# Running sums of the first two head pairs made in short runs, and the opening steps in another order

## Chip, core and metric

The kernel runs on one core of a Trainium2 chip. The metric is the device time of one execution in microseconds (us). The engines are named as in the profile: PE is the matrix engine TensorE, PEld its weight loads, DVE VectorE, ACT ScalarE, POOL GpSimd, SP the engine whose queue issues nearly all the DMAs.

## The reference, cut to what matters

Causal attention over 8 batches of 8 heads (576 positions, 64 wide), with a bias made from running sums of `s`; its output goes into a mixture of four experts, each an attention of its own, of which two are kept per position.

```python
cum = np.cumsum(np.maximum(s, 0.0), axis=-1)
bias = -(cum[:, :, :, None] - cum[:, :, None, :])
scores = np.where(causal, -1e9, q @ k.T / 8 + np.minimum(bias, 0.0))
attn = softmax(scores) @ v
x = attn.transpose(0, 2, 1, 3).reshape(B, S, H * D)
# then, for each expert e: softmax(causal(x @ wq[e] @ (x @ wk[e]).T / 8)) @ (x @ wv[e]) @ wo[e],
# weighted by a softmax over the two largest of x @ w_gate
```

## The kernel before

The 64 heads are worked in pairs, and so are the experts' attentions: 50 slots in all, 0 to 49. For a pair, the program makes the row maxima of the scores, then the scores and their exponentials, then the product with v. The scores of a pair are two products that add up: one (L688) over the low parts of q and k, the other (L693) over their high parts with extra rows below row 64. In those rows K2 holds the running sum of `s`, split into three terms that TensorE takes without loss, against rows of ones in Q2; one more row of Q2 holds minus the row maximum, against a row of ones in K2. So the running sum must be in place before a pair's maxima (L626), and the maxima before its scores. Q2 and K2 are rings of three buffers (`fill`, L349, sets their constant rows); Q1 and K1, with the low parts, are rings of two.

The order of the program is written out by hand in `STEPS`: a step `n:x` is step x of slot n, and each engine takes what it is given in that order. Steps that the prediction names, with the pair that slot n works on:

- `z0` to `z47`: an idle product on TensorE (L1340) whose result nothing reads; `FIRST_IDLE` such products stand ahead of all steps.
- `ld`, `lv`: loads of q and k (pair n+3) and of v (pair n). `hc` (pair n+2): running sums to K2 by DMA. `h0` to `h3` (pair n+2): high parts of q and k, on ACT.
- `lq`, `lk`, `l0`, `l1` (pair n+1): low parts. `lq` copies q on POOL, `lk` copies k on ACT, and `l0`, `l1` subtract (on DVE, and on POOL for one pair).
- `m0` to `m2` (pair n+2), `m3` to `m5` (pair n+1): maxima products, one PSUM bank each; `M0` to `M5` reduce the bank on DVE and give it back. `mt`, `mA`, `mq` (pair n+1): the maxima turned by TensorE, copied by ACT, and sent by two DMAs to the row of Q2.
- `s0` to `s6` and `E0` to `E6`: scores and their exponentials (pair n); `v0` to `v7`: product with v (pair n-1). `f1`, `f2`: `fill` of ring buffers 1 and 2. `cu` (slot -1): running sums to DRAM, for the pairs from 2 on. `lc`: constants, on POOL.

So pair 0 opens with slot -2, and `0:s4` is its first score product, `1:s4` that of pair 1. The running sums of all 64 heads are made at once (`running_sums`, L416): 64 partitions of 576 elements each, one scan along each of them on DVE, then the split in three.

Of the kernel before, what the change touches and what calls it, by code (L numbers as in the profile page):

```python
# [17 lines left out]
P = 128  # L18
# [12 lines left out]
FIRST_IDLE, IDLE = 32, 48  # L31
# [49 lines left out]
def heads(t, at, c0, c1):  # L81
# [240 lines left out]

COPY_Q, COPY_K = 3, 9

FB = [0, 8, 10, 12]
NQK1 = 2
NQK2 = 3
RC = 96
RM = 96


@with_exitstack
def tile_attention_then_moe(ctx, tc, qk, vm, vt, s, wqk, wvg, wo, out):
    nc = tc.nc
# [61 lines left out]
    def late_constants():  # L396
# [3 lines left out]
        for i in range(3):  # L400
            nc.gpsimd.memset(VB[i][64:128, :, 4], 0.0)
# [929 lines left out]
    def call(items):  # L1331
        for x in items:
            x()
# [118 lines left out]
```

## Time and profile before

| | us |
|---|---|
| median of 3 runs | 640.03 |
| lowest and highest run | 639.34, 640.57 |
| the profiled execution | 639.84 |
| its span, first to last instruction | 638.1 |
| PE busy in the span | 631.2 (99%) |
| DVE, ACT, POOL busy | 513.8, 445.2, 428.4 |

PE counts as busy also while it runs idle products, so the 99% tells nothing of useful work. The profile has a chain of work that ended last (followed back from the last instruction), a timeline of each engine, and windows that count one line's instructions in a stretch.

### The profile page before, as it was taken

The page shows a single profiled execution, that of the slowest core. Times are in us where ns is not written, and L with a number is a line of the kernel's source. Part 1 is how long each engine was busy: PE and PEld are TensorE (multiplying, and loading weights), DVE is VectorE, ACT ScalarE, POOL GpSimd, SP SyncE. Part 2 cuts the span into 40 slices and gives each one's busy share as a digit, 9 for nine tenths or more (in the row PEclk, how much of TensorE's full clock was granted, in tenths as well). Part 3 has the DMA queues.
Part 4 walks back from the last instruction along what each step waited for, and adds up shares of the span by engine and source line. Part 5 has one row for each costly group of instructions (what it writes and reads, how often), then busy time and mean ns, then how long its engine had stood idle before and what let it go on. Part 6 is the DMA issues. An engine that isn't in the chain of part 4 may idle for free.

```text
span 638.1 us, 16517 instructions
## 1 busy us (share of the span) xinstructions
PE 631.2 (99%) x5962; PEld 539.8 (85%) x5962; DVE 513.8 (81%) x1440; ACT 445.2 (70%) x974; POOL 428.4 (67%) x530
## 2 busy tenths in 40 slices
PE   9999999999999999999999999999999999999997
PEld 9888989789888888788897898788888889788875
DVE  8789788877989978895888778798887978763784
ACT  6697768866876676776768766785676776576354
POOL 8866598769864977487667766588676676828030
PEclk9999999999999999999999999999999999999999
DMA  5464643563565357445634454572563643432404
GB/s 167 132 186 133 182 111 79 143 141 96 159 162 136 91 150 188 145 130 134 182 100 132 129 130 134 156 200 76 141 193 87 157 130 88 111 101 64 103 1 148
DMA packets 61160, 83.39 MB, mean 131 GB/s; under 512 B 27063, under 2 KB 35623, under 8 KB 61079
## 3 DMA queue, kind: packets, MB, share of 16 engines
q1 hardware_dynamic: 60934, 82.21, 47.9%
q8 instruction: 47, 0.77, 0.5%
q14 instruction: 35, 0.28, 0.1%
q10 hardware_dynamic: 144, 0.13, 0.1%
HBM read 44.61 MB, written 10.16 MB: 86 GB/s over the span
## 4 chain that ended last, share of the span: by engine, by line
PE 97%; ACT 2%; DVE 1%; issue 0%; ACTq 0%
PE pvp L845 21%; PE pq L1080 16%; PE s L688 13%; PE s L693 12%; PE mx L626 10%; PE pw L1080 7%; PE po L1080 7%; PE sm L895 4%; PE idle L1340 3%; PE po L1049 1%; PE mt L661 1%; PE pw L1135 1%; PE pw L1140 1%; PE es L795 1%; PE gt L1249 0%; ACT p L709 0%
## 5 line engine op out<-in xcount | busy, mean ns | idle before, releaser
L709 ACT ACTIVATE p<-s 128x512 f32<-128x512 f32 x288 | 159.3, 589 | 40.8 <-PE s L693 32.3
L640 DVE CUSTOM_DVE_ANT_0 unread<-mx,mask 128x256 uint8<-128x256 f32 (+6 forms) x384 | 142.2, 419 | 33.9 <-PE mx L626 32.9
L688 PE MATMUL s<-q,k 128*128 128x288 f32 (+5 forms) x672 | 167.0, 285 | 0.5 <-issue 0.3
L693 PE MATMUL s<-q,k 97*128 97x288 f32 (+5 forms) x672 | 159.9, 279 | 0.0
L727 POOL TENSOR_SCALAR_AFFINE_SELECT p<-p 128x256 f32<-128x256 f32 (+2 forms) x183 | 109.5, 600 | 70.1 <-ACT p L709 67.7
L688 PEld LDWEIGHTS s<-q,k 128*128 128x128 f32 (+1 forms) x672 | 122.5, 183 | 7.5 <-issue 3.5
L774 POOL TENSOR_TENSOR r<-r,p 128x640 f32<-128x640 f32 x84 | 120.7, 1437 | 6.8
L693 PEld LDWEIGHTS s<-q,k 97*128 97x128 f32 (+1 forms) x672 | 121.7, 183 | 0.8
L845 PE MATMUL pvp<-p,v 128*64 128x320 f32 (+6 forms) x1024 | 99.5, 334 | 0.0
L600 DVE TENSOR_TENSOR q<-raw,q 64x576 fp32r<-64x576 f32 (+1 forms) x86 | 81.1, 952 | 22.5 <-ACT q L560 7.9
L605 DVE TENSOR_TENSOR k<-raw,k 64x576 fp32r<-64x576 f32 (+1 forms) x86 | 84.4, 991 | 5.5 <-DMA k<-k 3.4
L845 PEld LDWEIGHTS pvp<-p,v 128*64 128x64 f32 x1024 | 68.9, 136 | 22.7 <-ACT p L709 0.9
L626 PE MATMUL mx<-k,q 96*64 96x320 bf16 (+7 forms) x960 | 82.3, 293 | 0.9 <-DVE mcol L640 0.6
L1080 PE MATMUL pq<-xh,wqkh 128*128 128x288 f32 x256 | 76.4, 299 | 0.0
L1080 PE MATMUL pq<-xl,wqkh 128*128 128x288 f32 x256 | 75.6, 295 | 0.0
L1080 PE MATMUL pq<-xh,wqkl 128*128 128x288 f32 x256 | 75.4, 294 | 0.0
L768 POOL TENSOR_TENSOR r<-p 128x128 f32<-128x128 f32 x37 | 22.2, 600 | 72.3 <-ACT p L709 72.3
L626 PEld LDWEIGHTS <-q 96*64 96x64 bf16 x960 | 48.1, 109 | 22.1 <-issue 6.6
L563 ACT ACTIVATE k<-raw 64x576 fp32r<-64x576 f32 x96 | 64.8, 680 | 2.7 <-DMA raw<-in_qk_dram 0.6
L560 ACT ACTIVATE q<-raw 64x576 fp32r<-64x576 f32 x96 | 64.7, 681 | 1.9 <-PE s L693 0.4
L859 ACT ACTIVATE pv<-pvp 128x256 f32<-128x256 f32 (+1 forms) x92 | 36.1, 402 | 36.4 <-PE pvp L845 35.6
L1098 ACT ACTIVATE raw<-pq 128x288 f32<-128x288 f32 x64 | 25.4, 404 | 35.1 <-PE pq L1080 35.1
(159 smaller groups left out, 1265.5 us busy)
## 6 DMA issues: line engine op xcount, KB each, us to landing
raw<-in_qk_dram SPq DMA_DIRECT2D x30, 576.0 KB
rb<-rr SPq DMA_DIRECT2D x92, 144.0 KB
q<-q SPq DMA_DIRECT2D x45, 288.0 KB
k<-k SPq DMA_DIRECT2D x39, 288.0 KB
v<-in_vm_dram SPq DMA_DIRECT2D x32, 256.0 KB
out_dram<-o SPq DMA_DIRECT2D x31, 256.0 KB
q<-mr SPq DMA_DIRECT2D x96, 2.2 KB
raw<-in_qk_dram SPq DMA_DIRECT2D x4, 288.0 KB
```

What stands on the lines that cost most here:

```text
L563: nc.scalar.activation(k2[0:64, j], get_raw(n, j)[64:128], AF.Copy)
L600: eng.tensor_tensor(a[64:128, j], get_raw(n, j)[0:64], q2[0:64, j].bitcast(F32), op=OP.subtract)
L605: eng.tensor_tensor(c[0:64, j], get_raw(n, j)[64:128], c[64:128, j].bitcast(F32), op=OP.subtract)
L626: nc.tensor.matmul(t[64 * j : 64 * j + 64, c0 : c0 + k1 - k0], q2[0:RC, 64 * qt : 64 * qt + 64], k2[0:RC, k0:k1], start=True, stop=True,)
L640: nc.vector.tensor_tensor_reduce(t[:, 0:w] if len(MBANKS[bi]) == 1 else unread[:, c0 and 448 : (c0 and 448) + w], t[:, c0 : c0 + w], mask[ ...
L688: nc.tensor.matmul(t[0:nk, c0 : c0 + q1 - q0], K1[r1(n)][:, j, k0 : k0 + nk], Q1[r1(n)][:, j, q0:q1], start=True, stop=False,)
L693: nc.tensor.matmul(t[0:nk, c0 : c0 + q1 - q0], K2[r2(n)][0 : RM + 1, j, k0 : k0 + nk], Q2[r2(n)][0 : RM + 1, j, q0:q1], start=False, stop= ...
L709: nc.scalar.activation(chunk_of(ci, 0, 512)[:, x % 2], tl[x], AF.Exp, scale=0.125)
L727: nc.gpsimd.affine_select(out=a, in_=a, pattern=[[0, a.shape[1]], [1, w]], compare_op=OP.is_ge, fill=0.0, base=0, channel_multiplier=-1,)
L774: add(r[:, :, q0:S], r[:, :, q0:S], chunk_of(2, c, c + S - q0), op=OP.add)
L845: nc.tensor.matmul(cur[h][64 * j : 64 * j + 64, q0 - PVC[h] : q1 - PVC[h]], vsl(j, kt), heads(ptile[n], at, c, c + q1 - q0)[:, j], start=f ...
L1080: nc.tensor.matmul(t[0:nk, 0:w], l, r, start=(x == 0), stop=(x == len(terms) - 1))
```

## The change

`FIRST_IDLE` falls from 32 to 5; the 48 idle steps stay, some at other places. The running sums are made in two parts. `first_sums` takes the first four heads (pairs 0 and 1): each row of 576 is cut in 16 runs of 36, so that it lies on 32 partitions with two runs each; each run is scanned, a product with a triangle of ones gives what stands before each run, and that is added; the split in three follows on 72 columns. `running_sums` does all heads on 128 partitions, in two runs of 288, joined by a product with a matrix of zeros and ones (its three parts are the new steps `-2:cu`, `-2:cv`, `-2:cw`). The product is matrix `before` or `front`, built on POOL.

Four heads' sums reach K2 in one DMA of 96 pieces of 36 elements instead of two DMAs of three rows (`hc`, pairs 0 and 1). Later pairs read 12 half rows from DRAM. The extra rows close up: the row of minus the maxima moves from 96 to 67, so the products have 67 and 68 rows instead of 96 and 97, with the same columns. Buffer 0 of the rings is set by two ACT copies, buffers 1 and 2 by row transfers from it (two DMAs each on SP) in place of memsets of 32 partitions on POOL and DVE.

Of the steps, pair 0's loads alone come first and pair 1's load becomes a step (`-2:ld`); `l0`, `l1` of pair 0 go to POOL and those of pair 1 to DVE (the other way round before); pair 0's `mq` sends its second row from ACT's queue; `0:mq` stands right after `0:mA`; the constants of the gate leave `lc` for a new step `5:lg`. From `1:M3` on the steps are in their old order.

```diff
 SUMMED = 4
-FIRST_IDLE, IDLE = 32, 48
+FIRST_IDLE, IDLE = 5, 48
...
 STEPS = (
-    "-1:lk -1:ld -1:lq -2:h3 -2:z0 -2:z1 -2:h1 -2:z2 -2:z3 0:lq -2:z4 -1:l1 -2:hc -1:h0 -2:z5 -2:z6 "
-    "-2:z7 -2:h0 -2:h2 -1:l0 -2:m0 -2:m1 -2:M0 -2:m2 -1:f1 -1:m5 -1:m3 -1:m4 -2:z8 -2:z9 -2:z10 "
-    "-2:z11 -2:z12 0:f2 -2:M1 -1:h3 0:h3 0:lk -2:z13 -2:z14 -1:M3 -2:z15 -1:h2 -2:z16 -2:M2 -2:z17 "
-    "-2:z18 0:l1 -1:M5 0:h0 -1:M4 -2:z19 -1:h1 -1:cu -2:z20 -2:z21 -1:hc 0:m3 0:l0 -1:m2 -1:m0 0:m4 "
-    "0:h2 0:m5 -2:z22 0:M3 -1:mt -1:mA -1:M2 -1:m1 -2:z23 -2:z24 -2:z25 -2:z26 -2:z27 -2:z28 0:h1 "
-    "0:ld 0:hc -2:z29 -2:z30 0:m2 0:lv -1:mq 0:m1 0:s4 -1:M1 -1:M0 0:E4 1:lv 0:s2 0:s0 0:M5 0:s3 "
-    "0:M4 0:E2 0:lc 0:E0 0:s6 0:mt 0:mA 0:E3 0:M1 0:s5 0:E6 0:s1 0:E1 0:E5 1:m4 0:m0 1:m5 1:h1 1:m3 "
-    "1:h3 0:M2 -2:z31 1:v3 -2:z32 1:h0 1:M5 0:mq 1:M3 1:s4 0:d0 1:s2 1:s5 0:d2 1:E2 1:E5 1:s3 1:E3 "
-    "1:s1 1:M4 1:s0 1:h2 0:M0 1:mt 1:mA 1:E4 1:s6 1:hc 2:m5 1:v4 1:v5 0:d3 1:v6 1:E1 0:e0 1:l0 1:E0 "
...
+    "-2:hc -1:lq -2:cu -2:ld -2:h1 -2:h0 -2:z0 -2:z1 -2:z2 -2:z3 -2:z4 -2:z5 -2:z6 -2:cv -2:h3 -2:h2 "
+    "-2:cw 0:lc -2:z7 -2:z8 -2:z9 -2:z10 -2:z11 -2:z12 -2:z13 -2:m0 -2:m1 -1:lk -1:l1 -1:f1 -1:hc "
+    "0:f2 -1:h1 -2:M0 -2:m2 -1:m5 -1:m3 -1:m4 -1:l0 -2:M1 -1:ld -1:M3 -1:h0 -2:M2 -1:M5 -1:h3 -1:M4 "
+    "-1:h2 0:lq -1:cu 0:lv 1:lv -2:z14 -2:z15 -2:z16 -2:z17 -2:z18 -2:z19 -2:z20 -2:z21 -2:z22 "
+    "-2:z23 -2:z24 -2:z25 -2:z26 0:m3 -1:m2 0:lk 0:M3 -2:z27 -2:z28 -1:mt -1:mA -1:mq 0:ld -1:m0 "
+    "0:m4 -1:M2 0:m5 0:hc 0:h0 -1:m1 0:h2 -1:M1 0:h3 -1:M0 0:h1 0:M5 0:M4 0:s4 0:E4 0:s2 0:E2 0:s0 "
+    "0:E0 0:l1 0:mt 0:mA 0:mq 0:l0 -2:z29 -2:z30 0:m2 0:m1 0:s3 0:s6 0:E3 0:M1 0:s5 0:E6 0:s1 0:E1 "
+    "0:E5 1:m4 0:m0 1:m5 1:h1 1:m3 1:h3 0:M2 -2:z31 1:v3 -2:z32 1:h0 1:M5 1:M3 1:s4 0:d0 1:s2 1:s5 "
+    "0:d2 1:E2 1:E5 1:s3 1:E3 1:s1 1:M4 1:s0 1:h2 0:M0 1:mt 1:mA 1:E4 1:s6 1:hc 2:m5 1:v4 1:v5 0:d3 "
...
 NQK2 = 3
-RC = 96
-RM = 96
+RC = 67
+RM = 67
     def fill(i):
-        eng = nc.gpsimd if i else nc.vector
-        eng.memset(K2[i][64:96].bitcast(F32), 0.0)
-        eng.memset(Q2[i][64:96].bitcast(F32), 1.0)
-        nc.gpsimd.memset(K2[i][96:128].bitcast(F32), 1.0)
+        if i:
+            nc.sync.dma_start(Q2[i][64:67].bitcast(F32), Q2[0][64:67].bitcast(F32))
+        nc.sync.dma_start(K2[i][RM : RM + 1].bitcast(F32), Q2[0][64:65].bitcast(F32))
...
     nc.vector.memset(ones, 1.0)
-    fill(0)
...
+    before = PB[0][0:32, 0:32]
+    nc.gpsimd.memset(before, 1.0)
+    nc.gpsimd.affine_select(
+        out=before, in_=before, pattern=[[1, 32]], compare_op=OP.is_ge,
+        fill=0.0, base=-1, channel_multiplier=-1,
+    )
+    nc.gpsimd.memset(before[0:16, 16:32], 0.0)
+    nc.scalar.activation(
+        Q2[0][64:96].rearrange("p j s -> p (j s)"),
+        ones[64:96, 0:1].to_broadcast([32, 2 * S]), AF.Copy,
+    )
+    nc.scalar.activation(
+        K2[0][96:128].rearrange("p j s -> p (j s)"),
+        ones[96:128, 0:1].to_broadcast([32, 2 * S]), AF.Copy, scale=0.0,
+    )
...
     make_identity(nc, ident)
+    front = PB[0][:, 128:256]
...
     def late_constants():
-        nc.gpsimd.memset(vx[64:128, 4], 0.0)
...
+    def gate_constants():
+        nc.gpsimd.memset(vx[64:128, 4], 0.0)
     dram = ctx.enter_context(tc.tile_pool(name="dram", bufs=1, space=bass.MemoryType.DRAM))
-    cum = dram.tile([B * H, 3, S], F32, tag="cum", name="cum")
...
-    early = []
+    cum = dram.tile([2 * B * H, 3, HS], F32, tag="cum", name="cum")
...
+    early = {}
...
+    def rounded(hi, x):
+        nc.vector.tensor_single_scalar(
+            hi.bitcast(I32), x.bitcast(I32), -65536, op=OP.bitwise_and
+        )
...
+    def first_sums():
...
+        w = S // 16
+        st, rt, ct = (
+            sb.tile([P, S], F32, tag="pv", name=f"f_{c}", bufs=5)[0:32, 0 : 2 * w] for c in "trc"
+        )
+        c3 = PB[1][0:96, 1700 : 1700 + 2 * w]
+        s3, r3, c3 = (x.rearrange("p (n c) -> p n c", c=w) for x in (st, rt, c3))
+        early[0] = c3
+        t = {}
...
+        def begin():
+            nc.sync.dma_start(s3, s[0:4].rearrange("(n j) (c k) -> (j c) n k", n=2, k=w))
...
+        def scan():
+            nc.vector.tensor_scalar(rt, st, 0.0, 8.0, op0=OP.max, op1=OP.mult)
+            for n in range(2):
+                nc.vector.tensor_tensor_scan(
+                    r3[:, n], r3[:, n], r3[:, n], 0.0, op0=OP.add, op1=OP.max
+                )
...
+        def turn():
+            t[0] = take("cs0")
+            nc.tensor.matmul(t[0][0:32, 0:2], before, r3[:, :, w - 1], start=True, stop=True)
...
+        def split():
+            x = ct.rearrange("p (n c) -> p n c", c=w)
+            nc.vector.tensor_tensor(
+                x, r3, t[0][0:32, 0:2].unsqueeze(2).to_broadcast([32, 2, w]), op=OP.add
+            )
+            give(t[0])
+            rounded(c3[0:32], x)
+            nc.vector.tensor_tensor(c3[64:96], x, c3[0:32], op=OP.subtract)
+            rounded(c3[32:64], c3[64:96])
+            nc.vector.tensor_tensor(c3[64:96], c3[64:96], c3[32:64], op=OP.subtract)
+        return begin, scan, turn, split
     def running_sums():
-        n = B * H
-        st = sb.tile([P, S], F32, tag="pv", name="s_t", bufs=5)
-        nc.sync.dma_start(st[:n], s)
-        rt = sb.tile([P, S], F32, tag="pv", name="s_r", bufs=5)
-        nc.vector.tensor_scalar(rt[:n], st[:n], 0.0, 8.0, op0=OP.max, op1=OP.mult)
-        ct = sb.tile([P, S], F32, tag="pv", name="s_c", bufs=5)
-        nc.vector.tensor_tensor_scan(ct[:n], rt[:n], rt[:n], 0.0, op0=OP.add, op1=OP.max)
-        c3 = PB[1][:, 0:2400].rearrange("p (t c) -> p t c", c=800)[:, :, 0:S]
-        for j in range(2):
-            nc.vector.tensor_single_scalar(
-                c3[:n, j].bitcast(I32), ct[:n].bitcast(I32), -65536, op=OP.bitwise_and
-            )
-            o = c3[:n, 2] if j else ct[:n]
-            nc.vector.tensor_tensor(o, ct[:n], c3[:n, j], op=OP.subtract)
-        early.append(c3)
...
+        st, rt, ct = (
+            sb.tile([P, S], F32, tag="pv", name=f"s_{c}", bufs=5)[:, 0:HS] for c in "trc"
+        )
+        c3 = PB[1][:, 700:1660].rearrange("p (t c) -> p t c", c=320)[:, :, 0:HS]
+        early[1] = c3
+        t = {}
...
+        def begin():
+            nc.sync.dma_start(st, s.rearrange("h (c k) -> (h c) k", k=HS))
...
+        def scan():
+            nc.vector.tensor_scalar(rt, st, 0.0, 8.0, op0=OP.max, op1=OP.mult)
+            nc.vector.tensor_tensor_scan(rt, rt, rt, 0.0, op0=OP.add, op1=OP.max)
...
+        def turn():
+            t[0] = take("cs1")
+            nc.tensor.matmul(t[0][:, 0:1], front, rt[:, HS - 1 : HS], start=True, stop=True)
...
+        def split():
+            nc.vector.tensor_tensor(ct, rt, t[0][:, 0:1].to_broadcast([P, HS]), op=OP.add)
+            give(t[0])
+            for j in range(2):
+                rounded(c3[:, j], ct)
+                o = c3[:, 2] if j else ct
+                nc.vector.tensor_tensor(o, ct, c3[:, j], op=OP.subtract)
+        return begin, scan, turn, split
...
             if ph == 1 and n < 2:
-                for j in range(2):
-                    hd = 2 * i + j
-                    nc.sync.dma_start(k2[64:67, j].bitcast(F32), early[0][hd : hd + 1])
+                nc.sync.dma_start(k2[64:67].bitcast(F32), early[0][:, n])
             elif ph == 1:
-                hd = b * H + 2 * i
+                hd = 2 * (b * H + 2 * i)
                 nc.sync.dma_start(
-                    k2[64:67].bitcast(F32), cum[hd : hd + 2].rearrange("h t s -> t h s")
+                    k2[64:67].rearrange("p j (c s) -> p (j c) s", s=HS).bitcast(F32),
+                    cum[hd : hd + 4].rearrange("h t s -> t h s"),
...
             else:
-                nc.sync.dma_start(k2[64:67].bitcast(F32), k2[67:70].bitcast(F32))
+                nc.sync.dma_start(k2[64:67].bitcast(F32), K2[0][96:99].bitcast(F32))
         items["lq"], items["lk"] = copy_q, copy_k
-        eng = nc.gpsimd if n == 1 else nc.vector
+        eng = nc.gpsimd if n == 0 else nc.vector
...
             for j in range(2):
-                nc.sync.dma_start(
+                (nc.sync if n or not j else nc.scalar).dma_start(
...
         idle()
-    running_sums()
+    first, rest = first_sums(), running_sums()
+    first[0]()
+    rest[0]()
     call(load(0))
-    call(load(1))
+    fill(0)
+    for f in first[1:]:
+        f()
...
             steps["zz"] = lambda: give(idle_bank[0])
+        if n == -2:
+            steps["ld"] = lambda: call(load(1))
+            for x, f in zip("uvw", rest[1:]):
+                steps["c" + x] = f
...
             steps["f1"] = lambda: fill(1)
-            steps["cu"] = lambda: nc.sync.dma_start(cum, early[0][: B * H])
+            steps["cu"] = lambda: nc.sync.dma_start(cum, early[1])
...
             steps["lc"] = late_constants
+        if n == 5:
+            steps["lg"] = gate_constants
```

## Rows read from the trace of the kernel before

**Rows 1.** The page: chain of work that ended last, shares of the span by engine.

```profile
PE 97%; ACT 2%; DVE 1%; issue 0%; ACTq 0%
```

**Rows 2.** Windows, idle product (L1340) alone: stretch, length, PE busy (count), PEld, clock, DMA.

```profile
1.05:4.95 3.90, 3.90 (x19) 3.90 (x20) 1.00 0.72 212
5.10:9.00 3.90, 3.90 (x38) 3.90 (x37) 1.00 0.74 265
```

**Rows 3.** Timeline, running sums: start us, us, engine line op out<-in, forms, count [idle before].

```profile
0.81 0.58 SPq L419 DMA_DIRECT2D s_t<-in_s_dram  x1
0.88 0.11 DVE L357 MEMSET p<- 128x64 f32 x1 [0.88 <-PEq L1440]
...
3.72 0.45 DVE L421 TENSOR_SCALAR s_r<-s_t 64x576 f32<-64x576 f32 x1
4.20 1.35 DVE L423 TENSOR_TENSOR_SCAN s_c<-s_r 64x576 f32<-64x576 f32 x1
...
5.59 0.75 DVE L426 TENSOR_SCALAR p<-s_c 64x576 int32<-64x576 int32 x1
...
9.12 1.61 SPq L548 DMA_DIRECT2D k<-p  x2
...
11.86 1.56 PE L626 MATMUL mx<-k,q 96*64 96x448 bf16 x20
```

**Rows 4.** Timeline, the first loads and what ScalarE does with them.

```profile
0.80 1.28 ACT L591 ACT_TABLE_LOAD   x1 [0.80 <-PEq L1440]
...
1.44 2.00 SPq L509 DMA_DIRECT2D raw<-in_qk_dram  x4
...
4.37 0.68 ACT L591 ACTIVATE k<-raw 64x576 fp32r<-64x576 f32 x1 [2.28 <-DMA raw<-in_qk_dram]
...
6.83 0.68 ACT L591 ACTIVATE k<-raw 64x576 fp32r<-64x576 f32 x1 [1.78 <-DMA raw<-in_qk_dram]
```

**Rows 5.** Timeline, from the first maxima to the second pair's first score product.

```profile
12.52 0.62 DVE L640 CUSTOM_DVE_ANT_0 unread<-mx,mask 128x448 uint8<-128x448 f32 x1 [0.31 <-PE mx L626]
...
13.16 3.05 PE L1340 MATMUL idle<-p 128*64 128x128 f32 x26
...
15.54 0.70 SPq L522 DMA_DIRECT2D v<-in_vt_dram  x1
...
16.21 0.56 DVE L640 CUSTOM_DVE_ANT_0 mx<-mx,mask,mcol 128x320 f32<-128x320 f32 x1
...
17.65 0.28 PE L661 MATMUL mt<-p,mcol 128*9 128x128 f32 x1
...
17.96 0.27 ACT L665 ACTIVATE mr<-mt 9x128 fp32r<-9x128 f32 x1 [2.10 <-PE mt L661]
...
18.25 1.58 SPq L670 DMA_DIRECT2D q<-mr  x2
...
20.43 0.41 PE L688 MATMUL s<-q,k 128*128 128x320 f32 x1
...
25.80 0.42 PE L688 MATMUL s<-q,k 128*128 128x320 f32 x1
```

**Rows 6.** Timeline, low-part subtractions: VectorE for the first pair, GpSimd for the second.

```profile
9.12 1.71 DVE L605 TENSOR_TENSOR k<-raw,k 64x1152 fp32r<-64x1152 f32 x1
...
10.86 1.35 DVE L600 TENSOR_TENSOR q<-raw,q 64x1152 fp32r<-64x1152 f32 x1
...
16.10 2.65 POOL L605 TENSOR_TENSOR k<-raw,k 64x1152 fp32r<-64x1152 f32 x1
```

**Rows 7.** Chain that ended last, in order of time, where it leaves TensorE.

```profile
42.53 0.38 ACT pv L859
...
48.58 1.94 DVE q L600
```

**Rows 8.** Timeline of GpSimd: gate constants, and later the next pairs' copies of k.

```profile
21.40 0.31 POOL L397 MEMSET vx<- 64x260 f32 x1
...
78.23 1.15 POOL L586 TENSOR_SCALAR k<-raw 64x1152 fp32r<-64x1152 f32 x1 [7.00 <-PE s L693]
```

More of the change, by code (lines that the diff above doesn't have):

```diff
@@ L357, in tile_attention_then_moe @@
     nc.vector.memset(ones, 1.0)
-    fill(0)
+    before = PB[0][0:32, 0:32]
[13 more added lines that the diff above has]
+    )
     ident = PB[0][:, PSPARE : PSPARE + P]
     make_identity(nc, ident)
+    front = PB[0][:, 128:256]
+    nc.gpsimd.memset(front, 0.0)
+    nc.gpsimd.affine_select(
+        out=front[:, 1::2], in_=front[:, 1::2], pattern=[[-2, 64]], compare_op=OP.not_equal,
+        fill=1.0, base=0, channel_multiplier=1,
+    )
     gw = PB[1][:, PSPARE + D : PSPARE + D + 5 * E].rearrange("p (t e) -> p t e", e=E)
@@ new lines, in running_sums @@
+    def running_sums():
+        st, rt, ct = (
+            sb.tile([P, S], F32, tag="pv", name=f"s_{c}", bufs=5)[:, 0:HS] for c in "trc"
+        )
+        c3 = PB[1][:, 700:1660].rearrange("p (t c) -> p t c", c=320)[:, :, 0:HS]
[17 more added lines that the diff above has]
+        return begin, scan, turn, split
```

410 rows, old and new, of the table STEPS are left out of this document.

## The prediction

> **What bounds the kernel now.** I read the chain that ended last first: TensorE holds 97% of it [rows 1]. So a gain must take useless or waiting time out of TensorE's own queue, and it counts only if the queue has work ready when that time is gone. Then I read the timeline of the opening, because there TensorE runs idle products: they fill its queue from 1.05 us until the first maxima product at 11.86 [rows 2, 3]. Forty idle products stand there, two records each. Nothing useful is done on TensorE in these 10.8 us, and what it waits for is on the other engines. That is the only place where the change can gain; after the first steps the order is the same.
>
> What ends the opening: the rows of `s` go out at 0.81 and are read at 3.72; DVE scans 576 columns in 1.35 us and splits in four passes of 0.75 to 1.09, until the sums leave by two DMAs at 9.12 (1.61 us of issue for both); the first maxima product starts 2.74 us after that issue began [rows 3]. From there a chain of fixed length runs: reductions on DVE from 12.52 to 16.77, `mt` at 17.65, `mA` at 17.96, `mq` at 18.25, first score product at 20.43, and that of the next pair at 25.80 [rows 5]. I follow the change to this last event, 25.80, since from there the order is the old one.
>
> TensorE's clock is part of it. The granted clock reads 1.00 in both windows, but the idle product's records come 19 in the first 3.90 us and 38 in the next 3.90 us [rows 2]: half speed (1.2 GHz) until about 5.0, full speed (2.4 GHz) after. An idle product is about 0.42 us at the lower level; at the upper one it is 2 x 0.11 = 0.22, from 26 records in 3.05 us [rows 5].
>
> **The sums.** The new DMA for four heads is issued at 0.81 like the old one. It lands at most 2.9 us later (3.72 - 0.81, when DVE read the old one [rows 3]) and hardly below 1.9 (a sums DMA with its second issue at about 9.9 was used at 11.86); I take 3.4. Two scans of 36 columns, a pass of 72 and then five of 72: no row shows so short a pass. Below stands a 64-column one of 0.11, above the 0.75 of a full one [rows 3]; eight passes are 0.9 to 6 us. I take 0.15 each, near the short row: 0.45 before the product, 0.75 behind it. The product is a few columns: 0.11 to 0.42 by an idle record and a slow idle product; 0.3 with its two hand-overs. Sums ready at 4.95. The DMA of 96 pieces: 1.94 to 2.74 us by the same two readings of the sums DMAs, 2.15 taken, so it lands at 7.1. Before, it was needed at 11.86.
>
> **What then comes last: q and k.** ACT's table load ends at 2.08. The two constant copies on ACT are new; each is at most two of its 576-column copies, 2 x 0.68 [rows 4], so ACT is free at 4.7. Pair 0's first load is now second in line, issued at about 2.0, and lands 2.93 us after issue (4.37 - 1.44): 4.95. Four copies of 0.68 follow, the last two waiting for the second load. That landed by 6.83 among five loads [rows 4]; now it has fewer beside it, but leaves 0.5 later: 5.5 to 7.4. The copies end between 7.7 and 8.8. I take 8.1.
>
> **TensorE's queue.** Five slow idle products end at 3.15; it waits for the scan, does the product by 4.1; then 14 idle products and the second product (`-2:cv`). If the clock rises at about 5.0 as before, two slow and twelve fast ones and the product end at 7.8. So the first maxima start at 8.1, 3.8 us earlier than 11.86.
>
> **From there to the scores.** Three things must meet at `mt`. TensorE: six banks of maxima 1.30 (13.16 - 11.86), 13 idle products 2.9, two banks of pair 1 0.43, two idle 0.45: 13.2. DVE: 0.66 behind the first maxima, then 4.25 (12.52 to 16.77 [rows 5]): 13.0. ACT: two copies of k, four of pair 1, two more of k, each 0.68: 13.55. So `mA` starts at 13.6 instead of 17.96, and the first score product 2.47 later (20.43 - 17.96 [rows 5]) at 16.1.
>
> Two covers. The subtractions of pair 0 are now on POOL, 2.65 each by the row of pair 1 [rows 6]: from 9.5 to 14.8, hidden by 1.3 us; if that is gone, scores slip one for one. And SP, which is in order: behind pair 0's sums (issued 4.95 to 5.75) come 13 more DMAs ahead of `mq`: five of short rows at 0.8, two loads at 0.5, a load and the write to DRAM at about 0.5 each, and four of v at about 0.55 (the tail alone is 0.70), in all 8.2, so SP is free at 14.0 when `mA` ends at 13.9. That is no cover at all: if a row transfer costs more than 0.8, `mq` and the scores wait, five times the difference. Pair 0's second row on ACT's queue: no row shows an issue from ACT; 0 to 0.8 us of ACT, in front of pair 2's copies, not of the first score.
>
> **To the next pair's scores.** Before, 5.37 us (25.80 - 20.43). Two idle products (0.45) and two banks of pair 2 (0.43) now lie inside: 6.25, to 22.35. DVE: pair 0's reductions end at 13.0, pair 1's at 17.25 or 17.4, then pair 1's subtractions, 1.71 + 1.35 by the DVE rows [rows 6], to 20.4; then one bank for which `1:m5` waits: 21.1, against 20.9 on TensorE. That costs 0.1 to 0.5. Altogether 3.45 less 0.45 for this and the hand-overs: 3.0 us of gain.
>
> Edits at nothing: 67 and 68 rows instead of 96 and 97 (the columns set the product's length); `lc` without the gate's constants, and `5:lg` in slot 5, about ten short POOL instructions, the largest 0.31, in a stretch where POOL stands 7.00 us idle before its next copy of k [rows 8]; without that gap at most 1.2 us for POOL alone. The memsets that go lay on POOL and DVE beside the idle products.
>
> The old order is kept behind that point, so the gain should be carried on. One stretch is not TensorE's: from 42.53 to 50.5 the chain runs over ACT and DVE [rows 7]. Both keep their place relative to TensorE to within some 0.5 us, so I take nothing off.
>
> Sum: 639.84 (span 638.1, 1.7 around it) - 3.0 = 636.84. The profiled run is 0.19 below the median, so 637.0.
>
> **Rivals.** (A) *The clock rises late.* The early idle products did more than fill: TensorE ran without a break for 3.95 us before it went to 2.4 GHz [rows 2]. Now it stops from 3.15 to 3.8. If the 3.95 us count anew from the product at 4.1, the rise is at 8.05, the first maxima at 9.2, and everything behind 1.0 later: 638.0. For it: the gap; against it: the gap is short.
>
> The Trainium skill's page "TensorE: Matmul & The Clock Gate", section "What's actually happening", says that the throttled state is the default, that activity releases it, and that the observation does not start anew with the kernel; by that rule the rise is not bound to the first product, so this rival and the forecast are both open. Rows 2 agree on the throttled start.
>
> (B) *Slower than before.* The same mechanism at a higher price: each idle product at the lower level is 0.2 us longer and the maxima take twice as long, while 27 of them lie between the second sums and `mt`. If the rise comes at 13 us or later, nothing is left (first maxima 10.4, `mt` 16.8, next pair's scores 25.9). If it stays low until the scores, `mt` is at 20.3 and the kernel 3.6 us slower, 643.6. It decides from 13 us on.
>
> (C) *The short pieces don't do what they should.* If 96 pieces of 144 B, or the short passes, bring the sums in at 11 us instead of 7.1, 3 to 3.9 us are lost one for one: 639.8 to 640.7.
>
> By the skill's "DMA: Bandwidth & Descriptors", section "Bandwidth", transfers under 64 KB are dominated by their descriptors, which speaks for C. No row here has such pieces alone.
>
> (D) *The gain is handed back later*: SP's row transfers, the DVE subtractions or the stretch of [rows 7] eat 1 to 2 us: 638.0 to 639.0.
>
> (E) *More than forecast*: q and k land early and SP keeps up, 4 us: 636.0.
>
> **How the numbers follow.** Forecast 637.0, chance 0.42; A 0.19; D 0.14; E 0.08; C 0.10; B 0.07. A measurement of this kernel tells 0.2% (1.3 us) from no change. Below 638.75 lie the forecast, A, E and half of D: 0.76, I say 0.75; within: the other half of D and most of C, 0.15; slower 0.10. The range goes from 635.8 to 639.3: it leaves out B, C and the ends of E.
>
> **What would show it.** In the changed profile: the first maxima product at about 8 us (11.86 before); the count of idle records doubling near 5 us (forecast) or 8 us (A); the first score product at about 16, that of pair 1 at about 22.5; `mq` issued right at the end of `mA` (SP even) or later (D); the same distance from 1:s4 to the last instruction as before, 612.3 us, if nothing is handed back. I am wrong if the sums' DMA lands after 9 us, if TensorE is at half speed past 9 us, or if that distance grows.

## The result: 1% slower, and why one profile does not show it

| | executions | median, us | lowest, highest | mean granted clock |
|---|---|---|---|---|
| before | 20 | 640.25 | 639.34, 641.54 | |
| changed | 20 | 647.61 | 639.95, 649.29 | 0.980 to 0.996 |
| changed, the profiled one | 1 | 640.89 | span 639.2 | 0.993 |

The ratio is 1.0096, 95% interval 1.0073 to 1.0119: 1% slower and clear of the noise, where 637.0 was forecast. In this ratio and those further down (which are not quotients of the medians) an execution more than 1.5% above the fastest of its kernel is left out, which is one each in e2 (650.50) and e11 (649.56). The profiled execution is one of the quickest of the twenty, 1.05 us above the profiled one of before; the median lies 7.4 us above. So the profile has to show which mechanism is at work, and the list of executions what it costs.

The list is plain once the mean granted clock stands beside the time. The granted clock has two levels in these traces, 1.00 (2.4 GHz) and 0.50 (1.2 GHz), so a mean clock c over a span means 2 x (1 - c) x span at the lower one:

| execution of the changed kernel, us | mean clock | us at 1.2 GHz |
|---|---|---|
| 639.95 | 0.996 | 5.1 |
| 640.89 (the profiled one) | 0.993 | 8.9 |
| 644.24 | 0.989 | 14.1 |
| 647.30 | 0.981 | 24.5 |
| 649.29 | 0.980 | 25.9 |

A straight line through all twenty has a slope of 0.40 us per us at 1.2 GHz (correlation 0.93). The Trainium skill ("TensorE: Matmul & The Clock Gate", section "HAM oscillation — how this bites in real kernels") prices such time at half its length; the slope of 0.40 is near that. The time in the table is a little too large for the opening: at the very end, when TensorE has no work left, the clock falls too, and this costs nothing. Of the 8.9 us of the profiled execution 6.8 lie in the opening and 2 behind 637.1 us; before has 1.6 us there (0.50 from 636.5 on) and none in the opening once the clock is up. The executions of before beside the experiments show 0.997 to 1.0. They also show that the clock is not the only thing that varies: one of them took 646.60 with a mean clock of 0.999.

The opening of the changed kernel, from its timeline (start, duration, engine, line, operation, output<-inputs, forms, count, idle time before it and its releaser):

```profile
0.81 0.39 SPq L455 DMA_DIRECT2D f_t<-in_s_dram  x1
2.45 0.19 DVE L458 TENSOR_SCALAR f_r<-f_t 32x72 f32<-32x72 f32 x1 [1.45 <-DMA f_t<-in_s_dram]
3.38 0.26 PE L466 MATMUL cs<-f_r,p 32*32 32x2 f32 x2
4.63 0.58 DVE L477 TENSOR_TENSOR p<-p 32x72 f32<-32x72 f32 x1
5.23 0.91 SPq L622 DMA_DIRECT2D k<-p  x1
7.83 0.46 DVE L506 TENSOR_TENSOR s_c<-s_c,p 128x288 f32<-128x288 f32 x1
8.05 0.39 PE L701 MATMUL mx<-k,q 67*64 67x448 bf16 x1
8.59 2.62 POOL L680 TENSOR_TENSOR k<-raw,k 64x1152 fp32r<-64x1152 f32 x1 [0.96 <-ACT k L666]
8.66 2.87 DVE L506 TENSOR_TENSOR p<-s_c,p 128x288 f32<-128x288 f32 x1
11.45 0.61 DVE L715 CUSTOM_DVE_ANT_0 unread<-mx,mask 128x448 uint8<-128x448 f32 x1
13.80 1.42 SPq L597 DMA_DIRECT2D v<-in_vm_dram  x1
15.80 0.38 PE L736 MATMUL mt<-p,mcol 128*9 128x128 f32 x1 [2.17 <-DVE mcol L715]
16.22 0.27 ACT L740 ACTIVATE mr<-mt 9x128 fp32r<-9x128 f32 x1 [3.20 <-PE mt L736]
16.51 1.32 ACTq L745 DMA_DIRECT2D q<-mr  x1
18.73 0.63 PE L768 MATMUL s<-q,k 68*128 68x320 f32 x1 [0.29 <-DMA q<-mr]
26.98 0.42 PE L763 MATMUL s<-q,k 128*128 128x320 f32 x1
```

The first maxima stand at 8.05, against 11.86 [rows 3]. The lead is lost on the way in this execution: `mt` (L736) at 15.80 after TensorE has stood idle 2.17 us, the first product that needs the row of maxima (L768) at 18.73, pair 1's first score at 26.98, against 25.80 [rows 5]. From there to the last instruction it is 612.2 us; before 612.3.

The windows show what the stop does (stretch, length, busy time and count of PE, PEld, DVE, ACT, POOL, then granted clock, DMA share, GB/s):

```profile
13.40:15.80 2.40, 0.23 (x3) 0.00 (x1) 2.25 (x13) 0.00 (x0) 1.93 (x3) 1.00 1.03 351
15.83:22.66 6.83, 6.54 (x36) 4.80 (x38) 5.84 (x22) 4.48 (x9) 0.00 (x0) 0.50 0.48 148
22.70:26.00 3.30, 3.30 (x36) 2.78 (x33) 2.25 (x9) 1.48 (x4) 0.00 (x0) 1.00 0.01 1
```

First TensorE has 0.23 us of work in 2.40 us. Then, as it starts again, its clock is at 1.2 GHz and stays there 6.83 us although it is busy for 6.54 of them: the score product of 320 columns takes 0.63 us at 18.73, where 0.31 was its time before. Only then the clock is back. In 17 of the other 19 executions the mean clock gives 14 to 26 us at the lower level instead of 8.9; in the other two it gives 5.1, and they took 639.95 and 640.53.

### The profile page after: what moved, and what is told of

The parts are those of the page before. It is cut to its first block, busy times and chain, and to the rows that moved or that the text cites. A ratio compares the mean times of both kernels' runs of the same rounds, so it can differ in the third digit from the quotient of the medians.

```text
span 639.2 us, 16430 instructions
## 1 busy us (share of the span) xinstructions
PE 630.1 (99%) x5912; PEld 535.8 (84%) x5912; DVE 514.4 (80%) x1447; ACT 447.1 (70%) x976; POOL 420.1 (66%) x528
## 4 chain that ended last, share of the span: by engine, by line
PE 95%; DVE 2%; ACT 2%; issue 1%; DMA 0%; DVEq 0%; ACTq 0%
PE pvp L920 21%; PE pq L1155 16%; PE s L763 13%; PE s L768 12%; PE mx L701 10%; PE pw L1155 7%; PE po L1155 7%; PE sm L970 4%; PE po L1124 1%; PE mt L736 1%; PE idle L1415 1%; PE pw L1210 1%; PE pw L1215 1%; PE es L870 1%; DVE unread L715 0%
## 5 line engine op out<-in xcount | busy, mean ns | idle before, releaser
L768 PE MATMUL s<-q,k 68*128 68x288 f32 (+5 forms) x672 | 161.1, 280 | 0.3 <-DMA q<-mr 0.3
L768 PEld LDWEIGHTS s<-q,k 68*128 68x128 f32 (+1 forms) x672 | 122.5, 184 | 1.4 <-DMA q<-mr 0.6
L675 DVE TENSOR_TENSOR q<-raw,q 64x576 fp32r<-64x576 f32 (+1 forms) x86 | 82.7, 970 | 21.5 <-ACT q L635 7.9
L920 PE MATMUL pvp<-p,v 128*64 128x64 f32 (+6 forms) x1024 | 99.7, 334 | 0.1
L701 PE MATMUL mx<-k,q 67*64 67x320 bf16 (+7 forms) x960 | 83.5, 295 | 0.9 <-DVE mcol L715 0.6
L701 PEld LDWEIGHTS <-q 67*64 67x64 bf16 x960 | 48.4, 110 | 22.7 <-issue 6.7
```

The costliest lines, as they stand in the source:

```text
L675: eng.tensor_tensor(a[64:128, j], get_raw(n, j)[0:64], q2[0:64, j].bitcast(F32), op=OP.subtract)
L701: nc.tensor.matmul(t[64 * j : 64 * j + 64, c0 : c0 + k1 - k0], q2[0:RC, 64 * qt : 64 * qt + 64], k2[0:RC, k0:k1], start=True, stop=True,)
L768: nc.tensor.matmul(t[0:nk, c0 : c0 + q1 - q0], K2[r2(n)][0 : RM + 1, j, k0 : k0 + nk], Q2[r2(n)][0 : RM + 1, j, q0:q1], start=False, stop= ...
L920: nc.tensor.matmul(cur[h][64 * j : 64 * j + 64, q0 - PVC[h] : q1 - PVC[h]], vsl(j, kt), heads(ptile[n], at, c, c + q1 - q0)[:, j], start=f ...
```

## The experiments

My theory after this result: the stops of TensorE ahead of the first scores, which the prediction took for harmless waiting, let the clock fall, and the lower clock is the loss. Rivals: the loss comes from the waits alone (a late row of maxima); or from parts of the change that the profile shows nowhere near the opening. All times stand against the kernel before, run on the same chip beside each (640.3 to 640.6). Each kernel was executed ten times, e9 six times. e8, e9 and e10 ran on one chip, the other nine on another, so a comparison of e8 with e11 or e12 also crosses chips; e1, e2, e3, e5 and e11 can be compared on one.

| kernel | median, us | lowest, highest | ratio to before, 95% interval |
|---|---|---|---|
| e1: 11 idle products ahead of `mt` | 644.85 | 639.76, 648.56 | 1.0055, 1.0019 to 1.0091 |
| e10: 11 ahead of `mt`, 12 ahead of `0:s4` | 640.89 | 639.92, 641.99 | 1.0008, 0.9996 to 1.0020 |
| e4: before, with 5 first idle products | 643.02 | 641.84, 644.75 | 1.0025, 1.0001 to 1.0048 |
| e7: before, six idle products less | 640.35 | 638.90, 642.18 | 0.9994, 0.9980 to 1.0008 |
| e2: gate constants first | 647.30 | 640.57, 650.50 | 1.0079, 1.0044 to 1.0113 |
| e3: e2 and 8 idle products ahead of `0:s4` | 641.21 | 638.86, 647.86 | 1.0022, 0.9984 to 1.0060 |
| e6: loads of v later | 644.25 | 642.06, 648.45 | 1.0060, 1.0035 to 1.0084 |
| e5: e3 and loads of v later | 638.56 | 637.66, 645.71 | 0.9980, 0.9953 to 1.0007 |
| e8: e5 and `cu` earlier | 637.70 | 637.42, 642.32 | 0.9968, 0.9950 to 0.9985 |
| e9: e8 and 6 idle products ahead of `0:m2` | 637.85 | 637.47, 639.33 | 0.9958, 0.9942 to 0.9974 |
| e11: e8 without the 8 idle products | 643.18 | 638.50, 649.56 | 1.0043, 1.0012 to 1.0075 |
| e12: e8, subtractions as before | 641.66 | 640.87, 643.73 | 1.0025, 1.0014 to 1.0036 |

### Fill the stop, shorten nothing

e1 fills one stop, e10 both, with products whose result nothing reads; no wait is shortened. The cuts of code here and below show pieces of lines of `STEPS`; `IDLE` rises with the number of idle steps.

```diff
-    "-2:z27 -2:z28 -1:mt -1:mA -1:mq"
+    "-2:z27 -2:z28 -2:z48 -2:z49 -2:z50 -2:z51 -2:z52 -2:z53 -2:z54 -2:z55 -2:z56 -2:z57 -2:z58 "
+    "-1:mt -1:mA -1:mq"
```

> The changed kernel with eleven more idle products ahead of the first pair's `mt`, so that TensorE has no 2.4 us gap there; nothing else differs. Theory (clock): the loss is TensorE's clock, which falls at `mt` because the queue stands empty from 13.4 to 15.8 us, and in the 20 runs each us at the lower level costs about 0.45 us; filled, the clock stays up, all runs lie close together at 638.0 to 639.5. Rival (later work): SP's row transfers and VectorE's subtractions hand the gain back whatever the clock does; 646 to 648 as now. Rival (too few opening products): the clock is unsteady because only five stand ahead; runs stay spread from 640 to 649.

In e1 the stop at `mt` is gone, but the fall comes one wait later. Two pieces of its chain, then its windows:

```profile
15.72 0.22 PE mt L737
...
16.26 2.62 DMA q<-mr
```

```profile
16.30:18.90 2.60, 0.92 (x11) 0.49 (x7) 1.98 (x11) 1.26 (x2) 0.00 (x0) 1.00 0.49 107
19.00:32.66 13.66, 13.66 (x69) 11.30 (x69) 8.83 (x27) 6.64 (x13) 4.45 (x7) 0.50 0.36 123
33.00:40.00 7.00, 7.00 (x82) 5.54 (x85) 3.64 (x15) 6.74 (x14) 3.46 (x4) 1.00 0.16 46
```

While the row of maxima travels, TensorE works 0.92 of 2.60 us; then it runs 13.66 us at 1.2 GHz and is busy for all of them. The executions do not lie close together at 638.0 to 639.5, as was expected. Two executions of ten kept a clock of 0.998 or more, and these took 639.76 and 639.91. One filled stop doesn't do; so both:

```diff
+    "-2:z28 -2:z48 -2:z49 -2:z50 -2:z51 -2:z52 -2:z53 -2:z54 -2:z55 -2:z56 -2:z57 -2:z58 -1:mt"
...
+    "0:M4 -2:z59 -2:z60 -2:z61 -2:z62 -2:z63 -2:z64 -2:z65 -2:z66 -2:z67 -2:z68 -2:z69 -2:z70 0:s4"
```

> The changed kernel with eleven idle products more ahead of `mt` and twelve more ahead of the first score product: no wait is shortened, TensorE only has something to run during both. Theory (clock): the clock stays up in most runs, 638.0 to 639.5, against 647.6 for the changed kernel, though TensorE runs 5 us more of idle products. Rival (the delays themselves cost the time): 645 to 648, and by the idle products' own length still more.

```profile
13.40:15.80 2.40, 2.40 (x24) 2.40 (x22) 1.28 (x6) 0.00 (x0) 2.31 (x3) 1.00 1.04 368
15.83:22.66 6.83, 6.83 (x66) 5.88 (x65) 5.18 (x16) 4.47 (x9) 0.14 (x1) 1.00 0.50 143
```

These are the windows of e10 in the stretches where the changed kernel stood and then crept: full and at 1.00, with 66 records where 36 were. All ten executions have a clock of 0.999 or 1.0. Twenty-three products that compute nothing take the kernel from 647.6 to 640.9, so the loss is the clock, and the clock falls when TensorE's queue stands empty. At 640.89 it is still above the 638.0 to 639.5 that was expected: the products also hold `mt` back to 16.11, while the last reduction it needs had ended by 13.4, and the first score product to 19.93; that is why e10 only draws level.

### The same in the kernel before

e4 takes 27 idle products from the head of the kernel before and touches nothing else; e7 takes six from its later opening (those behind them move up in number).

```diff
-FIRST_IDLE, IDLE = 32, 48
+FIRST_IDLE, IDLE = 5, 48
```

> The kernel before with 5 instead of 32 idle products ahead of the steps, nothing else. Theory (clock): TensorE stands idle until about 12 us, the clock is low through the first scores and beyond; 644 to 650, spread. Rival (idle products only fill waiting time): 640.0, as before.

```profile
5.00:8.40 3.40, 1.02 (x9) 0.78 (x7) 3.26 (x5) 3.27 (x6) 3.40 (x4) 1.00 0.91 314
8.50:18.60 10.10, 6.91 (x41) 6.42 (x42) 7.82 (x23) 6.08 (x10) 9.76 (x9) 0.50 0.52 137
```

Windows of e4: the stop before the first maxima brings 10 us at 1.2 GHz and costs 2.65 us (643.02 against 640.37; less than the 644 to 650 that were expected, and just clear of the noise), though the first maxima come no later than before (11.45 against 11.86), since the sums set them. The 27 products were not only waiting time: they held the clock.

```diff
-    "0:h2 0:m5 -2:z22 0:M3 -1:mt -1:mA -1:M2 -1:m1 -2:z23 -2:z24 -2:z25 -2:z26 -2:z27 -2:z28 0:h1 "
+    "0:h2 0:m5 -2:z22 0:M3 -1:mt -1:mA -1:M2 -1:m1 0:h1 "
```

> The kernel before without the six idle products z23 to z28 that stand between `mt` and the first score product; every other step as it was. Theory (clock): TensorE stops for about 1.4 us where they stood, the clock falls in many runs and stays low for 7 us and more, 641 to 646, spread. Rival (idle products only fill waiting time, the clock does not mind so short a stop): 640.2, as before.

The fall that was expected didn't come: 0.9994, no change, and no execution below 0.998. The waits of TensorE between 7 and 30 us tell why (who waits, for whom, us in total, times, longest):

```profile
PE mx L626 <- DMA k<-p: 0.4, 1, 0.4
PE mx L626 <- ACT k L563: 0.3, 1, 0.3
PE s L693 <- DVE mcol L640: 0.2, 1, 0.2
```

The maxima of pair 2 and the first score product moved up into the gap (19.25 for 19.56, 19.82 for 20.43), and what was left are stops of 0.4 us and less. The clock stayed up.

### Take away what makes TensorE wait

e2 puts the gate's constants (`5:lg`) behind `0:lc`, ahead of POOL's subtractions, so that POOL comes later than VectorE's pass; e3 adds eight idle products; e5 moves the loads of v (`0:lv 1:lv`) behind pair 2's sums; e6 does that alone.

```diff
+    "-2:cw 0:lc 5:lg -2:z7"
...
-    "-1:h2 0:lq -1:cu 0:lv 1:lv -2:z14"
+    "-1:h2 0:lq -1:cu -2:z14"
...
-    "0:m5 0:hc 0:h0"
+    "0:m5 0:hc 0:lv 1:lv 0:h0"
...
-    "0:M4 0:s4"
+    "0:M4 -2:z48 -2:z49 -2:z50 -2:z51 -2:z52 -2:z53 -2:z54 -2:z55 0:s4"
...
-    "6:M5 5:lg 6:lk"
+    "6:M5 6:lk"
```

> The changed kernel with the gate's constants back at the end of `lc`, ahead of GpSimd's first subtraction, so that this one starts after VectorE's last pass of the split has begun. Theory (VectorE held by GpSimd, then clock): the last pass falls from 2.87 us to about 0.5, the first reduction starts at about 9.2 instead of 11.45, `mt` at about 13.5 without a gap, the first score product at about 16.3; a gap of some 1.7 us ahead of the scores stays, so 637.5 if the clock survives it, 640 to 645 if not. Rival (later work): the opening moves but 646 to 648 stays. Rival (the last pass is slow by itself, for its output's place): still near 2.9 us, and no change.

e2 removes one wait and keeps the loss. VectorE's pass is 0.46 us, the reductions start at 9.34 and TensorE doesn't wait for `mt` (VectorE's pass is 0.46 us in the profiles of e1, e6 and e10 too, without this edit, so it is not shown that the edit did it); the row of maxima, sent at 14.72 behind the loads of v, arrives as late as ever (chain; then TensorE's only wait; then the windows):

```profile
14.72 3.70 DMA q<-mr
```

```profile
PE s L768 <- DMA q<-mr: 3.0, 1, 3.0
```

```profile
17.10:40.90 23.80, 22.43 (x121) 18.54 (x123) 10.52 (x34) 11.86 (x24) 8.21 (x10) 0.50 0.26 85
```

Its median, 647.30, is above the 640 to 645 that were expected and is the number of the rival "later work". Its profile, of an execution of 647.62, decides against that rival. Copies of the maxima on ACT (`mA`) of the same two pairs, an early one and the last, from the timeline of before and then from that of e2:

```profile
47.72 0.25 ACT L665 ACTIVATE mr<-mt 9x128 fp32r<-9x128 f32 x1
...
600.86 0.27 ACT L665 ACTIVATE mr<-mt 9x128 fp32r<-9x128 f32 x1 [1.16 <-PE mt L661]
```

```profile
56.58 0.25 ACT L740 ACTIVATE mr<-mt 9x128 fp32r<-9x128 f32 x1
...
609.66 0.27 ACT L740 ACTIVATE mr<-mt 9x128 fp32r<-9x128 f32 x1 [1.16 <-PE mt L736]
```

The delay is 8.9 us at the first and 8.8 at the second: all that an execution as slow as the changed kernel's median loses is lost before 57 us, in the stretch that holds the 23.8 us at 1.2 GHz.

> As the kernel with the gate's constants ahead of GpSimd's subtraction, and eight idle products more ahead of the first score product, where TensorE would wait for the row of maxima. Theory (clock): no gap is left, the clock stays up, 636.8 to 638.0 in all runs. Rival (later work): 646 to 648. Rival (too few opening products): spread from 640 to 649.

Eight idle products and nothing else, on the same chip, take e2 from 647.30 to 641.21, though not to the 636.8 to 638.0 that were expected. The three executions of e3 that kept the clock took 638.86 to 639.25; its profiled one (644.09) shows the remaining stop. `mA` had ended at 14.39, but SP was still issuing v:

```profile
14.39 1.34 SPq L599 DMA_DIRECT2D v<-in_vt_dram  x1
...
15.83 0.85 SPq L746 DMA_DIRECT2D q<-mr  x1
...
18.55 0.41 PE L769 MATMUL s<-q,k 68*128 68x320 f32 x1 [1.40 <-DMA q<-mr]
```

> The changed kernel with the loads of v for pairs 0 and 1 moved behind the row of maxima, and nothing else. Theory (clock after a stop): the stop of 2.4 us at `mt` stays, where GpSimd holds VectorE's last split pass, so the clock falls all the same: 645 to 648, though the scores begin some 0.5 us earlier. Rival (the loads of v alone cost the time): 638 to 640.

The stop of 2.4 us at `mt` that was expected was not there in e6: POOL came behind VectorE's pass in its profile. With v later the row leaves at 14.71, and TensorE's stops are 0.9 and 0.7 us. Yet the clock was low for 20 us, from 17.7 on, and the median is 644.25 (the two stops in the timeline, then a window):

```profile
16.61 0.41 PE L768 MATMUL s<-q,k 68*128 68x320 f32 x1 [0.94 <-DMA q<-mr]
...
20.55 1.06 PE L701 MATMUL mx<-k,q 67*64 67x320 bf16 x8 [0.71 <-DMA v<-in_vm_dram]
```

```profile
17.70:38.10 20.40, 19.69 (x105) 15.91 (x105) 9.63 (x29) 10.53 (x21) 8.22 (x10) 0.50 0.34 111
```

The stop of 0.7 us came when the clock was already down. So one stop of 0.9 us stood before the fall, and TensorE had been at work again for 1 us.

> As the kernel with the gate's constants first and eight idle products ahead of the scores, and the loads of v for pairs 0 and 1 moved behind the row of maxima and the next load on SP. Theory (SP and the loads of v keep the row of maxima back, TensorE stops at the scores, the clock falls): the row goes out right behind `mA` at about 14.5 instead of 15.83, the wait of 1.4 us at the first high-part score product falls under 0.5, the clock stays up in most runs, 637.0 to 638.5. Rival (the clock falls for want of opening products): still spread, with a median of 641 and more. Rival (later work): 640 and more with the clock up.

e5 has e3's edits and the later loads of v, and seven of ten executions took 639.35 or less. One stop of 1.3 us is left, from a transfer that I had not priced: the running sums of pair 2 must be read back from DRAM behind their write, and everything behind that read on SP waits too (chain of e5):

```profile
10.95 6.68 DMA cum<-p
```

e8 lets the write go out right behind pair 1's sums:

```diff
-    "-1:lk -1:l1 -1:f1 -1:hc 0:f2 -1:h1"
+    "-1:lk -1:l1 -1:f1 -1:hc -1:cu -1:h1"
...
-    "-1:ld -1:M3 -1:h0"
+    "-1:ld 0:f2 -1:M3 -1:h0"
```

> As the kernel with late loads of v and eight idle products ahead of the scores, and the write of the later pairs' sums to DRAM moved up on SP, ahead of the second ring fill and the next load. There the third pair's sums were read back only at 17.69 us, 6.7 us after the write's issue, and TensorE stood 1.3 us at that pair's maxima. Theory (a stop of TensorE here lets the clock fall): the write goes out 1 to 1.5 us earlier, the stop falls under 0.5 us, nearly all runs keep the clock up, median 637.3 to 638.2. Rival (the clock falls by chance whatever the stops): again three of ten runs at 640 to 646, median 638.5.

```profile
9.19 0.63 SPq L1485 DMA_DIRECT2D cum<-p  x1
...
13.65 0.28 PE L737 MATMUL mt<-p,mcol 128*9 128x128 f32 x1
...
14.26 0.78 SPq L746 DMA_DIRECT2D q<-mr  x1
...
16.58 0.41 PE L764 MATMUL s<-q,k 128*128 128x320 f32 x1
...
24.10 0.41 PE L764 MATMUL s<-q,k 128*128 128x320 f32 x1
```

In this timeline of e8 `mt` is at 13.65 (forecast 13.2, with `mA` at 13.6, which came at 13.96), the row goes out when `mA` ends, and pair 1's first score comes 1.7 us before that of the kernel before. It beats both kernels: 637.70, or 2.6 us less than before, and its profiled execution (637.42) has a mean clock of 1.0. The stop at pair 2's maxima is 0.7 us instead of 1.3 (under 0.5 was expected). From pair 1's first score to the end it is 611.6 us instead of 612.3. Up to the last copy of maxima 0.3 us are lost (599.43 against 600.86, a lead of 1.4), behind it 1.0 is gained; no run tells why.

> As the kernel with the earlier write of the sums, and six idle products more ahead of the third pair's first maxima. Theory (clock): no stop is left at all, the clock stays up in every run, 637.3 to 638.5, at most 0.5 above the kernel without the six. Rival (idle products cost what they last): 1.3 us slower than without them, and no fewer slow runs.

Six more idle products change nothing in the median; the six executions all have 0.999 or more, where one of e8's ten fell to 0.994 and took 642.32.

### Take parts out of e8

e11 takes the eight idle products out. e12 keeps them and gives pair 0's subtractions back to VectorE and pair 1's to POOL.

> As the kernel with the gate's constants first, late loads of v and the earlier write of the sums, but without the eight idle products ahead of the first score product: the delays are shortened, nothing fills what is left. Theory (a stop of TensorE ahead of the scores lets the clock fall): some 1.7 us without work stay there, so the clock falls in a good part of the runs, median 640 to 645, spread over 5 us and more. Rival (the shorter delays are all that counts): 637.5 to 638, as with the eight.

e11: 643.18, from 638.50 with a clock of 0.997 to 649.56 with 0.982. Its profiled execution kept the clock and took 638.91, with stops of 1.3 and 0.9 us. So stops like these don't always bring the fall; no trace shows those of the executions that lost the clock. The eight products make the difference: e8 with them has 637.70, and e5, on the same chip as e11 and with the later `cu`, 638.56.

```diff
-        eng = nc.gpsimd if n == 0 else nc.vector
+        eng = nc.gpsimd if n == 1 else nc.vector
```

> As the kernel with the earlier write of the sums and the eight idle products, but the subtractions of pair 0 back on VectorE and those of pair 1 on GpSimd, as in the kernel before. Theory (the swap is what frees VectorE for the first reductions): 1.71 and 1.35 us of subtractions stand ahead of or among the first reductions, `mt` comes 2 to 3 us later, TensorE stops there, 640 to 645 with clock falls. Rival (the swap gives nothing, the shorter sums alone do): 637.7.

```profile
9.11 1.81 DVE L681 TENSOR_TENSOR k<-raw,k 64x1152 fp32r<-64x1152 f32 x1
10.96 0.62 DVE L716 CUSTOM_DVE_ANT_0 unread<-mx,mask 128x448 uint8<-128x448 f32 x1
...
11.77 1.35 DVE L676 TENSOR_TENSOR q<-raw,q 64x1152 fp32r<-64x1152 f32 x1
...
16.73 0.38 PE L737 MATMUL mt<-p,mcol 128*9 128x128 f32 x1 [3.08 <-DVE mcol L716]
```

Timeline of e12: the subtractions lie between the reductions (1.81 + 1.35), and `mt` comes 3.08 us later than in e8. 641.66, all ten above before's median; two executions kept a clock of 1.0 and still took 641.03 and 641.54, so here the delay itself costs too. Giving them to POOL is what lets VectorE be through at 13.4 in e8, where the prediction had 13.0.

## Why the prediction was wrong, step by step

- **The sums: right, in part by luck.** Forecast 4.95 and 7.1 for ready and landed; the DMA left at 5.23 and the first maxima ran at 8.05, forecast 8.1. Two errors cancel: the load of `s` was there at 2.45, 0.95 us earlier than taken, and passes and product took 1.2 us longer (the five short passes 0.18 to 0.58 us each, not 0.15). And the first maxima came behind TensorE's own idle products, not behind the copies of q and k, which ended at 7.23 and not at 8.1 (the two constant copies on ACT took 1.16 each, where the sum, 2.08 and four times 0.68, gives 4.8 for their end and not 4.7; they ended at 4.43). Each pair's sums (two heads, not four) go out in one DMA of 96 pieces. Rival C (pieces of 144 B too slow) is out: 2.82 us lie between issue and use, 2.74 before; both ways move 14 KB, so the size alone did not speak for C. So is A: twelve records of idle products take 1.54 us from 6.77 on, 0.13 each, against 14 in 2.72 us from 3.57 on; the rise lies between, not at 8.05.
- **VectorE 0.66 behind the first maxima: wrong in the profiled execution.** POOL's subtraction began at 8.59, VectorE's last pass of the sums at 8.66, and that pass took 2.87 us, until POOL was through; the same operation took 0.46 at 7.83. The reductions began at 11.45 instead of 8.71. In the profiles of e1, e6 and e10, with the same steps up to there, POOL began 0.3 to 0.9 us behind the start of that pass, and it took 0.46 us. So it is a matter of which one comes first. I had priced POOL's work by its own cover alone and not by whom it stops. The Trainium skill has the rule ("SBUF — State Buffer", section "SBUF: two separate sides": whichever of two such operations starts first keeps the shared ports to its end and the other is blocked wholly); these rows agree with it.
- **SP free at 14.0: 0.6 to 1.9 us short.** It was free at 14.62 in e2 and at 15.87 in the changed kernel. The ring fills were cheaper than taken (0.54 to 0.76 against 0.8). The tails of v were dearer: 0.55 had been taken, from a row of 0.70 [rows 5]; 1.02 and 1.44 stand in e1's profile, 1.34 in e3's. In the profile of the changed kernel `mA` was later still and SP did not count; in e3 it cost 1.4 us. "No cover at all" was the right remark, but the price put on it was only the delay.
- **The step that failed: a stop of TensorE, put at nothing beyond its own length.** The sum has TensorE at 2.4 GHz from about 5.0 us on. Between `mA` at 13.6 and the first score product at 16.1 it has TensorE wait for the row, with four banks of maxima and not one idle product to run, and counts this wait as already paid. In most executions the clock falls around this stop: behind it in the profiles of e1 and e3, within it in e2's, and in that of the changed kernel, where VectorE was held, already at `mt`. That cost 14 to 26 us at 1.2 GHz at 0.40 us each; with the stops filled (e10) the clock stayed up. The prediction named half speed past 9 us as a sign of being wrong, and that sign came. Rival B had this mechanism at about half its price (643.6, where the median is 647.61), and at the wrong place: it was tied to the first rise, which came on time, and so got a chance of 0.07.
- **The account of the profiled execution.** The sum said 636.84 and it took 640.89: 4.05 more. The wait at `mt` makes 2.6 (`mA` at 16.22 for 13.6). Half of the 3.9 us between the first product that needs the row (18.73) and the end of the lower clock (22.66) makes 2.0. The two come to 4.6; 0.2 comes back because this product follows `mA` by 2.51 us instead of 2.72, and the other edges, not traced one by one, must give the remaining 0.3 or so. That VectorE was held is particular to this execution: of the eleven profiles of the changed kernel and those made from it, it is the only one. The median's remaining 6.7 us (647.61 - 640.89) are the longer stretch at 1.2 GHz, as the table of executions, e2 and e10 show.
- **Handed back later (D): not in the sum.** 612.2 us from pair 1's first score to the end, 612.3 before. Inside, two parts cancel: up to the last copy of the maxima (602.92 against 600.86) 0.9 us are lost, and 1.0 is gained behind it, as in e8.
- **What was right for the kernel with its clock up:** e8 reached 637.70 where 637.0 was forecast. 2.6 of the 3.0 us are there, but only with five steps moved (`5:lg`, `0:lv`, `1:lv`, `-1:cu`, `0:f2`) and eight idle products put in. And the number is better than the working: the opening gained 1.7 us, since from the first score product to that of pair 1 it took 7.5 us (16.58 to 24.10), not 6.7, with a stop for pair 2's sums that was not in the sum. The other 0.7 in its profile (1.0 gained behind the last copy of the maxima, 0.3 lost on the way) was not forecast and is luck.

**What stays open:** why the clock takes between 7 and 24 us to return while TensorE is busy nearly throughout, and why stops of the same length bring the fall in one execution and not in another. How often POOL holds VectorE's pass in executions without a trace is not known. Leaving the ring fills as memsets, or sending both rows of maxima from SP, was not tried.

## What to carry to other kernels

Idle products ahead of the first steady stretch are worth their place beside every wait, not only at the start: ask of every wait on TensorE not only what it delays, but whether the queue is empty meanwhile, and fill it for as long as the wait may last, and not longer. Filler beside stops of 0.4 us (e7) or 0.7 us (e9) changed no median here. When an opening is shortened, move the filler with the waits, and follow the transfers of the last rows (here v and the running sums) on their queue. Judge by several executions with their clocks; a single profile here showed 640.9 for a kernel of 647.6.

## What the hardware showed unexpectedly

- The clock stays down for a long time after a fall, with TensorE busy nearly all the time: 13.66 us in e1 and 10.2 in e3 with no idle time, 6.8 in the changed kernel with 6.5 of them busy, and 23.8 in e2 with 22.4.
- No stop length divides falls from none: 0.9 us was followed by one in e6, 1.3 and 0.9 were not in e11's profiled execution, 0.4 and 0.3 were not in e7.
- An issue from ACT's queue took 1.32 us in the changed kernel, where the prediction had 0 to 0.8; SP's for the other row took 0.86. The prediction found no such row, but the trace of before has one at its end, for an output: 0.41 us at 634.02.
- A row of maxima that left behind the loads of v needed 3.70 us in e2; in the changed kernel, sent 1.8 us later, 2.17.
